# An mLSTM cell followed by a squared-ReLU feed-forward block: loads of later chunks, one chunk's normalisation and the in-place turns of x at other points of the instruction order

## The chip, the core and the metric

The kernel runs on one core of one Trainium2 chip. The metric is the device time of one execution in microseconds (us). A core has five engines that run side by side and meet through semaphores: PE (TensorE, the matmuls; its weight loads are listed as PEld), DVE (VectorE), ACT (ScalarE), POOL (GpSimd) and SP (SyncE, which here issues nearly all DMAs). Each engine works through its own list of instructions in the order in which the kernel's source issues them; an instruction that waits holds up all that stand behind it on the same engine. DMAs issued by SP are carried out by 16 DMA engines.

## The reference

```python
# mLSTM cell: batch 4, 8 heads, 768 steps, head dimension 40
for t in range(S):
    kt, vt, qt = (k[:, :, t], v[:, :, t], q[:, :, t])
    m_new = np.maximum(f_gate[:, :, t] + m, i_gate[:, :, t])
    f_stab = np.exp(f_gate[:, :, t] + m - m_new)
    i_stab = np.exp(i_gate[:, :, t] - m_new)
    m = m_new
    C = f_stab[:, :, None, None] * C + i_stab[:, :, None, None] * np.einsum('bhd,bhe->bhde', vt, kt)
    n = f_stab[:, :, None] * n + i_stab[:, :, None] * kt
    h_tilde = np.einsum('bhde,bhe->bhd', C, qt)
    nq = np.einsum('bhd,bhd->bh', n, qt)[:, :, None]
    denom = np.maximum(np.abs(nq), 1.0)
    o = 1.0 / (1.0 + np.exp(-o_gate[:, :, t]))
    y[:, :, t] = o * h_tilde / denom
# bridge: (4, 8, 768, 40) -> x of 3072 tokens x 320, then the feed-forward block, d_ff = 2048
h = np.maximum(x @ w_in, 0.0)
out = (h * h @ w_out).astype(np.float32)
```

## The kernel before

The 768 steps of each of the 4 batches are cut into 6 chunks of 128 steps, 24 chunks s = 0 to 23 in all. For each chunk the recurrence is worked out in matrix form: scores of k and q, weighted by decays (`W_sb`), times the values, plus the state C carried from chunk to chunk. Its result is normalised and gated into x, 128 tokens by 320. Two chunks make a token group g = s // 2 of 256 tokens, 12 groups in all, which goes through the feed-forward block: `ffn1` (x times w_in, L649 and L660), ReLU on ACT (L675), a square on DVE (L682), and the product with w_out (L743).

No scheduler reorders the work: the source writes out one order by hand, and each engine's list is that order. The first six chunks and the loading of the weights come first. From group g = 1 on, which starts at about 139 us, the order is a list `parts`, walked by n, and **a section of 8 parts belongs to each g** (r = n % 8 is the part in the section, b = 7 + 2 * (n // 8) a chunk number; g = 1 has n = 8 to 15 and b = 9, g = 2 has n = 16 to 23 and b = 11):

- parts 0 and 1: `ffn2_fast` steps 0 and 1 of group g
- parts 2 to 5: the four quarters of `ffn1` for group g + 2, with the scores and the attention of chunks b and b + 1 and b + 2 between them (`tiled`)
- parts 6 and 7: `ffn2_fast` steps 2 and 3 of group g

The sections of g = 10 and 11 have no `ffn1`. Before each part the source issues what stands ahead of it (chiefly work of DVE), and after it what stands behind it.

**`ffn2_fast`** makes the two row blocks y1 and y0 of group g with seven products in place of eight (sums of the squared activations, `sums`, L738, and of w_out, T). A product is 8 matmuls, 16 records in the trace. Products are written into PSUM tiles (`h_ps`), copied by ACT (L763, L768) or added by DVE (L759) into the tiles `y_sb`. There are three buffers of `y_sb`, used in turn: y1 of a group takes one, y0 the next. So y0 of group g + 1 lies in the buffer that y1 of group g had, and its first add (step 0) comes after the landing of y1's store. y1 is stored at the end of step 2 (L779, part 6), y0 at the end of step 3 (L784, part 7). The second product of step 1 overwrites a PSUM tile that the add of y0 in step 0 reads, and the products of steps 1 and 3 write to others that adds read.

**A chunk's way from attention to x** goes by DRAM, since it needs turns across partitions. `attend_turned(s)` leaves the numerators in `tn`; `store_num(s)` (L557) and `load_num(s)` (four DMAs, L562) bring them back in another arrangement. `normalise_turned(s)` (seven DVE instructions, L574 to L583) makes `x_sb`. `store_rows(s)` (L613) writes it to `x_rows` in DRAM, `load_rows(s)` (four DMAs, L618) reads it in blocks of 32 into a half of `xT` of its group, and `turn_squares(s)` (L625, DVE, in place) turns these blocks. `ffn1` of group s // 2 reads this `xT`; its first matmul of the main part is L649.

**Loads.** `load(s)` loads k and v of a chunk (L296, two DMAs), `load_o(s)` its output gate (L324), `load_A(s)` its decays, spread over the partitions (L334, 512 KB), `pair_up` and `load_squares(s)` bring q and k in 32 x 32 blocks (L287; four DMAs, L309). All of these and the stores stand on SP's list, in the order of the source.

In a section, SP's list before the change runs, from part 5 on: x's store of chunk b, the numerators' store and x's four loads of chunk b, the four loads of numerators of chunk b + 1, k and v of chunk b + 5, the gates of chunks b + 5 and b + 6, then y1's store (part 6), the four L309, y0's store (part 7), a load of A, and in the next section x's store and loads of chunk b + 1.

Of the kernel before, what the change touches and what calls it, by code (L numbers as in the profile page):

```python
# [29 lines left out]
def kernel(  # L30
# [536 lines left out]
    def normalise_turned(s):  # L567
        d = st[s]
        N = d["N"].rearrange("p (g e j r) -> p g e j r", g=2, e=2, r=SQ)
        R = D - SQ  # L570
        den = N[:, :, 1, :, R]
        dm = work.tile([P, H], F32, name="dm")
        dm2 = dm[:].rearrange("p (j g) -> p g j", g=2)
        nc.vector.tensor_scalar(dm2, den, scalar1=-1.0, scalar2=1.0, op0=ALU.mult, op1=ALU.max)  # L574
        nc.vector.tensor_tensor(dm2, dm2, den, op=ALU.max)
        nc.vector.reciprocal(dm[:], dm[:])
        x = d["x"] = work.tile([P, 3 * P], F32, name="x_sb")
        x3 = x[:, :DM].rearrange("p (h d) -> p h d", d=D)
        x4, og = x[:, :DM].rearrange("p (j g d) -> p g j d", g=2, d=D), d["og"].rearrange("p (j g) d -> p g j d", g=2)
        nc.vector.tensor_tensor(x4[:, :, :, :SQ], N[:, :, 0], og[:, :, :, :SQ], op=ALU.mult)  # L580
        nc.vector.tensor_tensor(x4[:, :, :, SQ:], N[:, :, 1, :, :R], og[:, :, :, SQ:], op=ALU.mult)
        nc.vector.tensor_tensor(x3, x3, dm[:].unsqueeze(2).to_broadcast([P, H, D]), op=ALU.mult)
        nc.vector.tensor_copy(x[:, DM:], x[:, DM - KR : DM])  # L583
# [27 lines left out]
    def store_rows(s):  # L611
        t = st[s]["xT"] = xT_half(s).rearrange("p c t -> p (c t)")
        nc.sync.dma_start(x_d[s].rearrange("c t d -> t c d"), st[s]["x"][:].rearrange("p (c d) -> p c d", c=3))  # L613

    def load_rows(s):
        t = st[s]["xT"]
        for r in range(P // SQ):
            nc.sync.dma_start(  # L618
                t[r * SQ : (r + 1) * SQ].rearrange("p (b a) -> p b a", a=SQ),
                x_d[s, :, :, r * SQ : (r + 1) * SQ].rearrange("c (n p) a -> p (c n) a", p=SQ),  # L620
            )
# [104 lines left out]
    def sums(g, ps, which=(1, 2, 3, 4)):  # L726

        if "S" not in st:
            st["S"] = [late.tile([P, NPAIR, P], F32, name=f"S{n}", bufs=1) for n in (1, 2, 4)]
        S1, S2, S4 = (t[:, ps] for t in st["S"])  # L730
        g4 = st["g2", g][:].rearrange("p (f two) t -> p f two t", two=2)[:, ps]
        A11, A12, A21, A22 = (g4[:, :, i, n * P : (n + 1) * P] for n in range(2) for i in range(2))
        for n in which:
            to, a, b, op = {
                1: (S1, A21, A22, ALU.add), 2: (S2, S1, A11, ALU.subtract),
                3: (A21, A11, A21, ALU.subtract), 4: (S4, A12, S2, ALU.subtract),
            }[n]
            nc.vector.tensor_tensor(to, a, b, op=op)  # L738
# [48 lines left out]
    def do(f, s):  # L787
        if 0 <= s < NT:
            f(s)

    def score(s):
        scores(s)
        weighted(s)
# [202 lines left out]
    def masked_W(s):  # L996
        weigh(s, masked=True)

    ALL = slice(0, NPAIR)
    for n, (which, g, i) in enumerate(parts):  # L1000
        s, at = 6 + n // 4, n % 4

        r, b = (n % 8, 7 + 2 * (n // 8)) if n >= 8 else (None, None)
        if n == 5:
            brought.close()
            late = ctx.enter_context(tc.tile_pool(name="late", bufs=1, side="right"))
        if n in (0, 4, 8):
            score(s)
            if n == 4:
                square_half()  # L1010
                square_half()
        if n in (2, 5):
            attend_turned(s)
            decays(s + 1)
            mask(s + 1)
            if n > 4:
                turn_kq(s + 1)
            decay_C(s + 1)
            if s > X_SQ:
                turn_squares(s - 1)  # L1020
            attended(s, early=(n == 5))
        if n == 6:
            scale_q(s + 1)
        if 5 <= n < 8:
            sums_of_weights(n - 5)
        if n == 6:
            sums(1, ALL, (1, 2))
        if n == 8:
            load_squares(10)
            load_A(10)  # L1030
            sums_of_weights(3)
            sums(1, ALL, (3,))
        if n == 9:
            score(9)
            attend_turned(8)
            decay_C(9)
            attended(8)
            turn_squares(7)

        if r == 0 and g > 1:  # L1040
            do(turn_squares, b - 2)
            sums(g, ALL, (3,))
        elif r == 4:
            do(scale_q, b + 1)
            do(turn_kq, b + 2)
        elif r == 5:
            do(normalise_turned, b)
            do(store_rows, b)
        elif r == 7 and g < NG - 1:
            sums(g + 1, ALL, (2,))  # L1050
        if g == NG - 2 and which == 2 and i == 3:
            sums(g + 1, ALL, (2,))
        if which == 2 and g == NG - 1 and i == 0:
            sums(g, ALL, (3,))

        if which == 1:
            ffn1_main(g, i)
            if i % 2 == 0:
                st["held"] = st["half"]
            elif r is None:  # L1060
                ffn1_batch(g, i)
                if n != 3:
                    square_half()
                    square_half()
            else:
                x = b + i // 2

                def tiled():
                    do(score, x + 1)
                    do(attend_turned, x)  # L1070

                ffn1_batch(g, i, tiled)
                do(decay_C, x + 1)
        elif g == 0:
            ffn2(g, *divmod(i, 2))
        else:
            ffn2_fast(g, i)

        if n in (2, 6):
            masked_W(s + 1)  # L1080
            if n < 4:
                turn_kq(s + 1)
                scale_q(s + 1)
            normalise_turned(s)
            store_rows(s)
            if n == 2:
                load_squares(s + 2)
            load_rows(s)
            if n == 2:
                load_A(s + 2)  # L1090
        if n == 7:
            for t in range(8, 12):
                sigmoid(t)
            decays(9)
            mask(9)
            turn_kq(9)
        if n == 8:
            masked_W(9)
        elif n == 9:
            load_A(11)  # L1100
            load_o(12)
            load_o(13)
            decays(10)
            mask(10)
        elif n == 10:
            normalise_turned(8)
            store_rows(8)
        if r == 0 and g > 1:
            do(decays, b + 1)
            do(mask, b + 1)  # L1110
            square_half()
            do(normalise_turned, b - 1)
            do(store_rows, b - 1)
        elif r == 1:
            if g > 1:
                do(load_rows, b - 1)
                do(pair_up, b + 2)
            square_half()
            if g < NG:
                sums(g, ALL, (4,))  # L1120
            do(scale_q, b)
            do(turn_kq, b + 1)
        elif r == 2:
            do(masked_W, b + 1)
            do(load_squares, b + 2)
            if n == 10:
                load_rows(8)
        elif r == 3:
            do(decays, b + 2)
            do(mask, b + 2)  # L1130
            attended(b)
            if b % 4 == 3:
                for t in range(b + 1, min(b + 5, NT)):
                    sigmoid(t)
        elif r == 4:
            square_half()
            square_half()
            do(masked_W, b + 2)
            do(load_A, b + 3)
            if b > 9:  # L1140
                do(turn_squares, b - 1)
        elif r == 5:
            do(store_num, b + 1)
            do(load_rows, b)
            do(load_num, b + 1)
            do(load, b + 5)
            for t in range(b + 5, min(b + 7, NT)):
                load_o(t)
        elif r == 6:
            do(load_squares, b + 3)  # L1150
            if n == 14:
                turn_squares(8)
        elif r == 7:
            do(load_A, b + 4)
        if which == 2 and g == NG - 1 and i == 0:
            sums(g, ALL, (4,))
        if n < 5:
            while rounding.done < LAST[n]:
                rounding.step(ahead=rounding.done + 1 < LAST[2])
# [30 lines left out]
```

## Time and profile before

| | us |
|---|---|
| median of 4 runs | 529.32 (528.5 to 534.61) |
| the profiled execution's own time | 528.5 |
| its span, first to last instruction | 526.7 |
| PE busy | 509.9 (97%) |
| PEld busy | 449.0 (85%) |
| DVE busy | 333.3 (63%) |
| ACT busy | 193.4 (37%) |
| POOL busy | 90.1 (17%) |
| DMA packets on SP's queue, share of 16 engines' span | 60.4% |
| granted clock of TensorE, mean | 0.993 |

The profile is of one execution. Its times are counted from the span's start. A row of the waits reads: who waited, for whom, us in total, times, longest. A row of the timeline reads: start, length, engine, line, operation, what is written and read, and in brackets how long the engine sat idle before and what ended that. Rows of SP are the issues of DMAs; a DMA lands some us after its issue. A row of the stretches reads: from and to, length, busy time of each engine with the number of instructions, the granted share of TensorE's clock, and the DMA engines' share and rate.

### The profile page before, as it was taken

Reading aid. Unit: us, or ns where it says so; the run is one execution under the profiler, and the core shown is the slowest. Engines: PE = TensorE matmul, PEld = TensorE weight load, DVE = VectorE, ACT = ScalarE, POOL = GpSimd, SP = SyncE. Lnnn points to the kernel's source line nnn. Section 1 sums busy time; section 2 is a strip of 40 time slices with the busy share of each in tenths; the row PEclk is TensorE's granted clock in tenths of the full one; section 3 lists DMA queues with packets and bytes.
Section 4 is the critical chain, followed back from the end, with each engine's and each line's share of the span. In section 5 each row is a group of like instructions: output and inputs, shape, how many; then the busy total and the mean of one; then the engine's idle time right before and its main releaser. Section 6 shows DMA issues by size and latency. Waiting matters only on the chain.

```text
span 526.7 us, 10339 instructions
## 1 busy us (share of the span) xinstructions
PE 509.9 (97%) x3933; PEld 449.0 (85%) x3933; DVE 333.3 (63%) x638; ACT 193.4 (37%) x460; POOL 90.1 (17%) x110
## 2 busy tenths in 40 slices
PE   9998999989999979999999999989999999999997
PEld 5876788877888878998898888988898898998997
DVE  8579988679866644754855845745865864431451
ACT  3786587362644123532334422333522301102000
POOL 3346553232321100010210211000210100000000
PEclk9999999999999979999999999999999999999999
DMA  9999698877679584785684774775664221200000
GB/s 196 227 201 210 149 201 200 191 175 149 149 152 180 138 167 78 167 143 112 168 147 101 172 135 110 178 137 118 148 153 75 72 79 36 64 12 1 26 26 26
DMA packets 239394, 68.06 MB, mean 129 GB/s; under 512 B 185744, under 2 KB 233872, under 8 KB 239344
## 3 DMA queue, kind: packets, MB, share of 16 engines
q1 hardware_dynamic: 239248, 67.20, 60.4%
q8 instruction: 31, 0.51, 0.4%
q10 hardware_dynamic: 96, 0.20, 0.1%
q14 instruction: 19, 0.16, 0.1%
HBM read 55.08 MB, written 17.86 MB: 138 GB/s over the span
## 4 chain that ended last, share of the span: by engine, by line
PE 64%; DMA 12%; SPq 11%; DVE 6%; ACT 3%; issue 3%; POOL 1%; DVEq 0%; POOLq 0%; ACTq 0%
PE h_ps L649 22%; PE h_ps L743 19%; PE h_ps L660 6%; DMA x_rows<-x_sb 4%; PE h_ps L689 3%; PE tp L424 3%; DMA out_dram<-y_sb 3%; SPq L562 3%; SPq L618 2%; SPq L324 2%; SPq L309 2%; PE numT L534 2%; DMA num_rows<-tn 1%; PE idle L802 1%; ACT W_sb L383 1%
## 5 line engine op out<-in xcount | busy, mean ns | idle before, releaser
L649 PE MATMUL h_ps<-xT,w_in 128*128 128x256 f32 x768 | 173.1, 383 | 1.8 <-POOL w_in L215 0.9
L649 PEld LDWEIGHTS h_ps<-xT,w_in 128*128 128x128 f32 x768 | 144.5, 191 | 23.5 <-issue 1.4
L675 ACT ACTIVATE r_sb<-h_ps 128x512 f32<-128x512 f32 x96 | 49.8, 599 | 112.0 <-PE h_ps L660 58.1
L743 PE MATMUL h_ps<-w_out,g 128*128 128x160 f32 x528 | 79.1, 306 | 6.3 <-DVE y_sb L759 6.2
L743 PEld LDWEIGHTS h_ps<-w_out,g 128*128 128x128 f32 x528 | 75.0, 194 | 7.8 <-DVE y_sb L759 7.5
L682 DVE TENSOR_TENSOR g<-r_sb 128x512 f32<-128x512 f32 x96 | 66.4, 741 | 10.0 <-ACT r_sb L675 10.0
L383 ACT ACTIVATE W_sb<-A_bc,b_T 128x128 f32<-128x128 f32 x176 | 53.8, 388 | 24.6 <-POOL A_bc L359 24.4
L437 DVE TENSOR_TENSOR P_sb<-tp,W_sb 128x512 f32<-128x512 f32 x46 | 29.7, 685 | 51.2 <-PE numT L534 33.5
L743 PE MATMUL h_ps<-T,S 128*128 128x160 f32 x352 | 52.3, 302 | 0.0
L743 PEld LDWEIGHTS h_ps<-T,S 128*128 128x128 f32 x352 | 48.8, 190 | 1.6 <-issue 0.9
L660 PE MATMUL h_ps<-xT,w_in 64*128 64x256 f32 x384 | 49.0, 391 | 0.0
L660 PEld LDWEIGHTS h_ps<-xT,w_in 64*128 64x128 f32 x384 | 34.8, 186 | 12.1 <-issue 9.1
L759 DVE TENSOR_TENSOR y_sb<-y_sb,h_ps 128x160 f32<-128x160 f32 x44 | 14.1, 320 | 44.4 <-PE h_ps L743 44.4
L763 ACT COPY y_sb<-h_ps 128x160 f32<-128x160 f32 x11 | 3.2, 293 | 99.5 <-PE h_ps L743 99.5
L359 POOL TENSOR_SCALAR_AFFINE_SELECT A_bc<-A_bc 128x1024 f32<-128x1024 f32 x22 | 27.2, 1236 | 73.5 <-ACT kq L369 64.3
L396 POOL TENSOR_TENSOR vw<-va,W_sb 128x328 f32<-128x328 f32 x20 | 17.4, 870 | 76.2 <-ACT W_sb L383 62.4
L490 POOL TENSOR_TENSOR Cd<-C,kq 128x164 f32<-128x164 f32 x15 | 6.9, 463 | 120.0 <-DVE C L551 105.7
L759 DVE TENSOR_TENSOR y_sb<-h_ps,y_sb 128x160 f32<-128x160 f32 x11 | 3.6, 324 | 37.1 <-DMA out_dram<-y_sb 23.8
L424 PEld LDWEIGHTS tp<-kqT 40*128 40x128 f32 x384 | 24.8, 188 | 2.4 <-issue 1.1
L743 PE MATMUL h_ps<-w_out,S 128*128 128x160 f32 x176 | 25.8, 300 | 0.8 <-DVE y_sb L759 0.8
L424 PE MATMUL tp<-kqT 40*128 40x128 f32 x384 | 26.1, 275 | 0.0
L743 PE MATMUL h_ps<-T,g 128*128 128x160 f32 x176 | 25.7, 299 | 0.0
(119 smaller groups left out, 609.7 us busy)
## 6 DMA issues: line engine op xcount, KB each, us to landing
A_bc<-a_rows SPq DMA_DIRECT2D x23, 512.0 KB, 4.9
raw<-in_moe_w_out_dram SPq DMA_DIRECT2D x16, 320.0 KB, 3.8
num_rows<-tn SPq DMA_DIRECT2D x18, 256.0 KB, 2.4
kq<-num_rows SPq DMA_DIRECT2D x72, 64.0 KB, 2.1
kqT<-kq_rows SPq DMA_DIRECT2D x34, 128.0 KB, 3.1
raw<-in_moe_w_in_dram SPq DMA_DIRECT2D x8, 512.0 KB, 5.2
kq<-in_k_dram SPq DMA_DIRECT2D x24, 160.0 KB, 3.9
va<-in_v_dram SPq DMA_DIRECT2D x24, 160.0 KB, 4.6
```

The source lines that it names most:

```text
L359: nc.gpsimd.affine_select(A[:], A[:], compare_op=ALU.is_ge, fill=-1e30, base=0, pattern=[[0, H], [1, P]], channel_multiplier=-1,)
L383: nc.scalar.activation(d["W"][:, i * n + h, :], A[i][:, h, :], AF.Exp, bias=b_T[:, b, c, i * n + h : i * n + h + 1],)
L396: nc.gpsimd.tensor_tensor(d["vw"][:], d["va"][:], d["W"][:, :, P - 1 : P].to_broadcast([P, H, D1]), op=ALU.mult,)
L424: nc.tensor.matmul(sc[i][:, j, :], lhsT=d["kT"][rows, j, :], rhs=d["qT"][rows, j, :], start=True, stop=True,)
L437: nc.vector.tensor_tensor(t, d["sc"][i], d["W"][:, heads, :], op=ALU.mult)
L562: nc.sync.dma_start(N[m * SQ : (m + 1) * SQ].rearrange("p (e c) -> p e c", c=P), n_d[s, :, m * P : (m + 1) * P].rearrange("(e p) c -> p e ...
L649: nc.tensor.matmul(hs[i][:, n, :], lhsT=w_in[:, a, fb * P : (fb + 1) * P], rhs=xT[:, :, a, :], start=(n == 0 and a == 0), stop=False,)
L660: nc.tensor.matmul(hs[i][:, n, :], lhsT=w_in2[rows, 2 * pp + n, :], rhs=xT[rows, :, 2, :], start=False, stop=(n == 1),)
L675: nc.scalar.activation(rs[-1][:], h[:], AF.Relu)
L682: nc.vector.tensor_tensor(g4[:, :, i, :], r[:], r[:], op=ALU.mult)
L743: nc.tensor.matmul(to, lhsT=lhsT[:, p], rhs=rhs[:, p, :], start=(start and p == 0), stop=(p == NPAIR - 1), skip_group_check=True,)
L759: add = lambda to, a, b: nc.vector.tensor_tensor(to, a, b, op=ALU.add)
```

## The change

Three things change places in the written order; no instruction is added or taken away.

- `load(b + 5)` and the two `load_o` go from the end of part 5 to the end of part 6, and so behind y1's store (L779) on SP's list. This is in effect in sections that still have chunks to load, g = 1 to 5.
- For chunk 9 alone, `normalise_turned` and `store_rows` go from ahead of part 5 in section g = 1 (n = 13) to behind part 6 (n = 14), and its `load_rows` from behind part 5 to behind part 7 (n = 15).
- `turn_squares(b - 2)` goes from ahead of part 0 to ahead of part 1 of a section, and the sum (3) stays ahead of part 0. On DVE's list the turn now stands behind the add of y0, two squares and the normalisation of chunk b - 1. `turn_squares(8)` stays in part 6 and stands behind chunk 9's normalisation there.

```diff
@@ ahead of a part
         if r == 0 and g > 1:
+            sums(g, ALL, (3,))
+        elif r == 1 and g > 1:
             do(turn_squares, b - 2)
-            sums(g, ALL, (3,))
         elif r == 4:
             do(scale_q, b + 1)
             do(turn_kq, b + 2)
-        elif r == 5:
+        elif r == 5 and b > 9:
             do(normalise_turned, b)
             do(store_rows, b)
@@ behind a part
         elif r == 5:
             do(store_num, b + 1)
-            do(load_rows, b)
+            if b > 9:
+                do(load_rows, b)
             do(load_num, b + 1)
+        elif r == 6:
+            if n == 14:
+                normalise_turned(9)
+                store_rows(9)
             do(load, b + 5)
             for t in range(b + 5, min(b + 7, NT)):
                 load_o(t)
-        elif r == 6:
             do(load_squares, b + 3)
             if n == 14:
                 turn_squares(8)
         elif r == 7:
             do(load_A, b + 4)
+            if n == 15:
+                load_rows(9)
```

SP's list in the changed kernel, from y1's store of section g = 1 to x's loads of chunk 9: L779, L613 (x of chunk 9), two L296, two L324, four L309, L784, L334, four L618 (x of chunk 9); then L613 and four L618 of chunk 10.

## The prediction

> **What bounds the kernel now.** I read the page's busy shares, then the waits of TensorE alone, then the busy time of each engine in chosen stretches, then the SP queue and the chain of waits where TensorE stands still.
>
> ```profile
> PE 509.9 (97%) x3933; PEld 449.0 (85%) x3933; DVE 333.3 (63%) x638; ACT 193.4 (37%) x460; POOL 90.1 (17%) x110
> ```
> ```profile
> PE h_ps L743 <- DVE y_sb L759: 7.0, 5, 3.2
> ```
> ```profile
> DVE y_sb L759 <- DMA out_dram<-y_sb: 23.8, 5, 5.4
> ```
>
> TensorE is busy for 97% of the span: time can only come from its gaps or from clock lost behind them. From 130 us on it waits for one thing alone, 5 times, 7.0 us: the adds of y (L759), which wait for the landing of an earlier store of y (23.8 us in 5 waits). A section's y0 takes the buffer that the section before stored as y1, through L779. The stretches below are part 1 of sections g = 2 to 7 (32 matmul records), then the halves behind the longest gap; the columns are the length, busy time by engine, the granted clock, DMA share and GB/s.
>
> ```profile
> 186.83:196.83 10.00, 6.76 (x35) 6.52 (x34) 3.74 (x11) 2.63 (x9) 0.91 (x1) 0.75 0.91 166
> 231.35:236.19 4.84, 4.62 (x34) 4.38 (x33) 2.55 (x9) 2.44 (x9) 0.70 (x1) 1.00 1.01 163
> 270.76:275.46 4.70, 4.62 (x35) 4.38 (x33) 2.56 (x9) 2.30 (x8) 0.65 (x1) 1.00 0.85 142
> 310.03:315.70 5.67, 4.61 (x34) 4.37 (x33) 2.55 (x9) 2.64 (x9) 0.00 (x0) 1.00 1.03 166
> 349.37:355.67 6.30, 4.61 (x34) 4.37 (x33) 2.55 (x9) 2.65 (x9) 0.69 (x1) 1.00 0.94 163
> 390.25:394.59 4.34, 4.34 (x34) 4.34 (x33) 3.10 (x10) 1.95 (x7) 0.64 (x1) 1.00 0.50 151
> ...
> 192.40:196.83 4.43, 4.43 (x17) 4.43 (x18) 3.14 (x9) 2.23 (x8) 0.91 (x1) 0.50 0.85 165
> 196.83:204.69 7.86, 7.86 (x34) 6.48 (x33) 4.42 (x6) 0.00 (x0) 0.00 (x0) 0.89 0.47 110
> ```
>
> Undisturbed, part 1 takes 4.34 us (g = 7, whose predecessor has no k, v or gates to load). In g = 2 it takes 10.00: 3.24 us of gap, then half clock. The clock is 0.50 for 4.43 us and 0.89 over the next 7.86, which is 1.73 us more at half: 6.16 us at half speed, 3.08 us lost, for a gap of 3.24. The gap of 1.69 us in g = 6 cost no clock. Why the store lands late is seen in SP's queue at the end of section g = 1:
>
> ```profile
> 183.61 1.84 SPq L562 DMA_DIRECT2D kq<-num_rows  x4
> 185.54 0.39 SPq L296 DMA_DIRECT2D kq<-in_k_dram  x1
> 186.04 0.53 SPq L296 DMA_DIRECT2D va<-in_v_dram  x1
> 186.62 2.43 SPq L324 DMA_DIRECT2D og<-in_o_gate_dram  x2
> 189.15 0.86 SPq L779 DMA_DIRECT2D out_dram<-y_sb  x1
> 190.06 2.90 SPq L309 DMA_DIRECT2D kqT<-kq_rows  x4
> 193.06 0.51 SPq L784 DMA_DIRECT2D out_dram<-y_sb  x1
> 193.67 0.38 SPq L334 DMA_DIRECT2D A_bc<-a_rows  x1
> 195.70 0.37 SPq L613 DMA_DIRECT2D x_rows<-x_sb  x1
> ```
>
> The add that L779 needs is done by 181.7, yet the store is issued at 189.15 and lands 2.75 us later by the chain, behind the loads of k, v and gates.
>
> **Loads behind the store (sections g = 1 to 5).** Nothing is added: L779 passes two L296 and two L324, 3.6 us of issue (185.54 to 189.15). The store lands about 3 us sooner, and the longest gap in g = 3 to 6 is 1.69. The four excesses over 4.34 go: 0.50 + 0.36 + 1.33 + 1.96 = 4.15 us gained. The loads come 0.4 to 0.9 us later; the values are first multiplied more than a section of 39 us on, so this costs nothing, and even without that cover less than 1 us a section. Bounds are 3.6 and 4.15: in g = 5 the store could be issued at 346.1, where k's load was, and even with the longest landing of the view, 4.5 us, it is there at 350.6, ahead of 351.7, where TensorE came to stand; I allow 0.1 us of waiting left in each of five.
>
> **Tenth chunk (s = 9), on VectorE.** Its seven instructions (L574 to L583, 175.44 to 177.25, 1.8 us) leave the place where they waited 3.81 us for their load, ahead of chunk 11's weighting. The store of the numerators (L557) needs only the weighting and the turn behind these, and goes from 179.28 to about 176.9. The add of part 6 no longer holds TensorE for 0.83 us: the product of 177.04 to 180.20 takes 3.16 us against 2.18 elsewhere, 0.98 gained. In the new place, 1.8 us behind part 6's last add, turn and S2 (0.5 + 1.2) end at about 183.3, and the product that reads S2 starts at 183.5: covered by 0.2 us; if not, some tenths.
>
> So TensorE reaches the first matmul of ffn1 in section g = 2 at 196.83 - 5.66 (10.00 less 4.34) - 0.98 = 190.2. It reads xT of chunks 8 and 9.
>
> **Tenth chunk, on the SP queue.** One store of x (L613) and four loads (L618, 1.86 us) move; the queues of POOL and ACT issue nothing here. Before, the loads are issued at 181.65 and chunk 9's turn ends at 185.95. Now L613 stands behind L779, and the four L618 behind L613, k, v, two gates, four L309, L784 and A's load. I walk the queue. L557 at 176.9 follows A_bc (issued 176.27) through the DMA engines, landing about 181.4, since A_bc landed at 181.1 with more beside it; four L562 end at 183.3; L779 is issued at 183.3 and lands before 186, y0's add needing it at 185.9 and TensorE at 187.9. From the end of L562 to A's load the queue took 193.67 - 185.45 = 8.2 us; with L613's 0.4 this is 191.9. The four L618 are issued from 192.4 to 194.3. They can't land before A: a median of 4.9 us from issue (section 6 of the page), 196.8; chunk 10's x store, issued at 195.70 behind an A of 193.67, released its loads at 199.10, 0.5 us after that A's 4.9. Their 196 KB add about 1 us at the 166 GB/s of that stretch: 197.8. Turn and two handovers, 0.7: 198.5.
>
> [...]
>
> So TensorE stands from 190.2 to 198.5, 8.3 us, a longer gap than the one removed; VectorE's turn waits with part 1's add, two squares, S4, the scaling of q and a turn behind it, some 4.8 us of work that scores at 209 need: covered. The price of clock: nothing (as behind 1.69 us) to 3.1 us (as behind 3.24 us); nearest is the second, so 3.1. The 32 matmuls, 7.00 us elsewhere, end at 198.5 + 7.0 + 3.1 = 208.6 instead of 204.69: 3.9 us lost, all earlier gains in this section counted.
>
> [...]
>
> Bounds: if the DMA engines hold up no issue (both gates at 0.6, as at 160.93, 1.2 us less; four L309 at 0.45, 1.1 less) and x lands 1.8 us after its last issue (xT's least), the turn ends at 194.0; with 4.2 (xT's longest) and a queue 1 us later, at 200.5. With 0 to 3.1 of clock the local change runs from 3.7 us won to 5.9 lost.
>
> **An x turn a part later (g = 2 to 9).** The 0.57 us of L625 move behind y0's add, two squares and a normalisation. Section g = 7 shows what there is between them and TensorE's need:
>
> ```profile
> 390.50 0.33 DVE L759 TENSOR_TENSOR y_sb<-h_ps,y_sb 128x160 f32<-128x160 f32 x1 [2.49 <-PE h_ps L743]
> 390.74 1.29 DVE L682 TENSOR_TENSOR g<-r_sb 128x512 f32<-128x512 f32 x2
> 393.55 0.20 DVE L583 COPY x_sb<-x_sb 128x64 f32<-128x64 f32 x1
> ...
> 394.59 0.59 PE L649 MATMUL h_ps<-xT,w_in 128*128 128x256 f32 x2
> ```
>
> The turn would run from 393.7 to 394.3, 0.3 us ahead of L649: nothing lost, 0 to 0.3 in each of six sections as bounds (1.8).
>
> **Sum.** The profiled execution took 528.5 us: a span of 526.7 and 1.8 around it. 528.5 - 4.15 + 3.9 = 528.3. The median of the four runs shown is 529.32, 0.8 above this execution, so no change that a run could tell; a measurement here tells about 1% (5.3 us).
>
> **Rivals.** (a) Chunk 9 is no obstacle: xT is turned by 190.2. Then 6.64, the 0.86 us of clock in L649 and 4.15 are won: 516.9. Against it: eleven DMAs stand between L779 and the first L618. (b) The queue runs freely, turn at 194.0: a gap of 3.8 us, matmuls done at 204.1 with 3.1 of clock, 0.6 won there: 523.8; without the loss of clock 520.7. For it: the store of numerators is out of the tangle; against it: a DMA share of 0.91 in that stretch. (c) Slower: the turns hold TensorE in each section. A normalisation in part 0 that waits for its numerators passes each us over 0.3 on to L649. VectorE has waited 5 times, 12.0 us, for such loads; five waits of 2.4 us, less 0.3 each, cost 10.5: 538.8. It decides from a wait of 0.3 us on. Against it: all five waits stood at other parts, none in part 0.
>
> **How the numbers follow.** Forecast 0.70, (a) 0.05, (b) 0.13, (c) 0.12. The forecast's own range is 524.5 to 531.5 (both ends of xT and of clock, not all at once). The range, 523.5 to 532.0, takes in (b) with its clock and leaves out (a), (c) at its full price and (b) without, about 0.2. Faster by over 1% means under 524.0: (a) and most of (b), 0.15. Slower by over 1%, over 534.6: 0.11, most of (c). Within: 0.74.
>
> **What would show it.** Right: part 1 at 4.34 us in g = 3 to 6; L779 at about 183; the first L649 of g = 2 waits some 8 us for L625, which waits for xT, and the clock halves again there. Wrong: no wait of PE for xT (a, b), or gaps ahead of L649 in later sections (c), or y's adds that still wait for out_dram.

## The result, and the profile after

| | before | after |
|---|---|---|
| median us (runs) | 530.82 (64) | 532.81 (43) |
| lowest to highest | 524.22 to 535.72 | 529.70 to 537.09 |
| ratio, 95% interval | | 1.0059 (1.0044 to 1.0074) |

The ratio leaves out as slow the runs more than 1.5% above their kernel's fastest, 19 of before's 64 and none of after's; over all runs the medians lie 2.0 us apart, 0.4%. So the change made the kernel slower by 0.4 to 0.6%, 2.0 to 3.1 us, where the prediction's sum had 0.2 gained. The profiled execution of after took 534.48 us, its span 532.7. First the busy shares of its page:

```profile
PE 513.7 (96%) x3933; PEld 450.5 (85%) x3933; DVE 332.8 (62%) x638; ACT 194.4 (36%) x460; POOL 91.8 (17%) x110
```

The waits of TensorE from 130 us on (who waited, for whom, us in total, times, longest):

```profile
PE h_ps L649 <- DVE xT L625: 10.6, 2, 9.8
PE h_ps L743 <- DVE y_sb L759: 0.5, 2, 0.3
```

The wait for y's adds has all but gone, from 7.0 us to 0.5; among VectorE's waits the adds wait for a store of y twice, 7.1 us in all, where it was 5 times, 23.8. In its place stands one wait of 9.8 us for the turned x, and a small one. The stretches of after: part 1 of g = 2, 3 and 6, and the first 32 matmuls of `ffn1` in g = 2 (length, busy time by engine, granted clock, DMA share, GB/s):

```profile
188.74:203.59 14.85, 4.78 (x34) 4.29 (x32) 4.15 (x12) 2.64 (x9) 0.78 (x1) 0.81 0.85 159
239.65:243.99 4.34, 4.34 (x34) 4.34 (x33) 3.65 (x11) 1.94 (x7) 0.69 (x1) 1.00 1.16 144
...
356.18:361.54 5.36, 4.51 (x35) 4.27 (x33) 3.65 (x12) 2.74 (x9) 0.69 (x1) 1.00 1.04 185
203.59:212.97 9.38, 9.38 (x32) 7.64 (x32) 4.25 (x6) 0.00 (x0) 0.00 (x0) 0.75 0.54 89
```

Part 1 takes the undisturbed 4.34 us in g = 3 (4.35 in g = 4 and 5), but 14.85 in g = 2, and 5.36 in g = 6. SP's list shows where the 9.8 us come from (start, length, line, what is written and read):

```profile
185.80 1.74 SPq L562 DMA_DIRECT2D kq<-num_rows  x4
187.64 0.38 SPq L779 DMA_DIRECT2D out_dram<-y_sb  x1
188.12 1.63 SPq L613 DMA_DIRECT2D x_rows<-x_sb  x1
...
192.68 3.51 SPq L309 DMA_DIRECT2D kqT<-kq_rows  x4
...
197.98 2.21 SPq L618 DMA_DIRECT2D xT<-x_rows  x4
```

x of chunk 9 is stored at 188.12, and its loads are issued only at 197.98, behind ten other DMAs. The last of these, A's load, is issued at 197.55 and lands at 201.87; the four loads of x land from 202.24 to 202.88. So x landed behind A, as the prediction's walk had it: in the profiles of before and after each of SP's 471 DMAs lands behind the one issued before it (neighbours on the list report through different ones of eight semaphores, so the order can be read). VectorE's turn and TensorE's list show the rest (idle time before, and what ended it, in brackets):

```profile
202.96 0.58 DVE L625 STREAM_TRANSPOSE xT<-xT 128x384 f32<-128x384 f32 x1 [8.30 <-DMA xT<-x_rows]
```
```profile
203.59 9.45 PE L649 MATMUL h_ps<-xT,w_in 128*128 128x256 f32 x32 [9.77 <-DVE xT L625]
```

Where the 6.0 us between the two spans went, counted from the first product of a section's part 1 to the next one's:

| us | before | after | difference | predicted |
|---|---|---|---|---|
| start to part 1 of g = 1 (same instructions in the same order) | 146.6 | 149.4 | +2.8 | 0 |
| g = 1 and 2 (chunk 9, first longer gap) | 84.76 | 90.25 | +5.5 | +3.9 |
| g = 3 to 6 | 158.90 | 156.57 | -2.3 | -4.15 |
| from part 1 of g = 7 to the end of the products | 133.3 | 133.3 | 0 | 0 |

The first row is not the change's. Without it the two executions differ by 3.2 us, the 0.6% of the ratio; a second profile of each (e9, e10) gives 376.8 and 380.1 us for that stretch, against 377.0 and 380.2. Before's stretch isn't that short in every execution: e7, which has the order of before from part 1 of g = 1 on, took 383.8 us for it, on a chip where the median of before is 534.34, with 12.1 us of waits for y.

### The profile page after: what moved, and what is told of

Read it like the earlier page. It is cut to its first block, busy times and chain, and to the rows that moved or that the text cites. A ratio compares the mean times of both kernels' runs of the same rounds, so it can differ in the third digit from the quotient of the medians.

```text
span 532.7 us, 10333 instructions
## 1 busy us (share of the span) xinstructions
PE 513.7 (96%) x3933; PEld 450.5 (85%) x3933; DVE 332.8 (62%) x638; ACT 194.4 (36%) x460; POOL 91.8 (17%) x110
## 5 line engine op out<-in xcount | busy, mean ns | idle before, releaser
L649 PE MATMUL h_ps<-xT,w_in 128*128 128x256 f32 x768 | 177.6, 390 | 12.5 <-DVE xT L625 10.6
L649 PEld LDWEIGHTS h_ps<-xT,w_in 128*128 128x128 f32 x768 | 147.3, 195 | 36.0 <-DVE xT L625 11.4
L743 PE MATMUL h_ps<-w_out,g 128*128 128x160 f32 x528 | 75.8, 300 | 0.3 <-DVE y_sb L759 0.3
L743 PEld LDWEIGHTS h_ps<-w_out,g 128*128 128x128 f32 x528 | 72.9, 190 | 0.8 <-DVE y_sb L759 0.6
L743 PE MATMUL h_ps<-T,S 128*128 128x160 f32 x352 | 52.3, 302 | 0.0
L743 PEld LDWEIGHTS h_ps<-T,S 128*128 128x128 f32 x352 | 48.7, 190 | 1.6 <-issue 0.9
L359 POOL TENSOR_SCALAR_AFFINE_SELECT A_bc<-A_bc 128x1024 f32<-128x1024 f32 x22 | 28.6, 1301 | 81.2 <-ACT kq L369 76.7
L316 DVE STREAM_TRANSPOSE kqT<-kqT 128x1024 f32<-128x1024 f32 x17 | 21.0, 1237 | 10.6 <-DMA kqT<-kq_rows 10.5
L424 PEld LDWEIGHTS tp<-kqT 40*128 40x128 f32 x384 | 24.8, 188 | 2.6 <-issue 1.4
L424 PE MATMUL tp<-kqT 40*128 40x128 f32 x384 | 26.3, 276 | 0.0
L369 ACT ACTIVATE kq<-A_bc 64x512 f32<-64x512 f32 x30 | 18.8, 628 | 20.4 <-DMA A_bc<-a_rows 18.6
L743 PE MATMUL h_ps<-w_out,S 128*128 128x160 f32 x176 | 25.8, 300 | 0.2 <-DVE y_sb L759 0.2
```

The lines of the kernel that those rows point to most:

```text
L316: nc.vector.transpose(t, t)
L359: nc.gpsimd.affine_select(A[:], A[:], compare_op=ALU.is_ge, fill=-1e30, base=0, pattern=[[0, H], [1, P]], channel_multiplier=-1,)
L369: nc.scalar.activation(e[rows], st[s]["A"][0][rows, PR * i : PR * (i + 1), :], AF.Exp)
L424: nc.tensor.matmul(sc[i][:, j, :], lhsT=d["kT"][rows, j, :], rhs=d["qT"][rows, j, :], start=True, stop=True,)
L649: nc.tensor.matmul(hs[i][:, n, :], lhsT=w_in[:, a, fb * P : (fb + 1) * P], rhs=xT[:, :, a, :], start=(n == 0 and a == 0), stop=False,)
L743: nc.tensor.matmul(to, lhsT=lhsT[:, p], rhs=rhs[:, p, :], start=(start and p == 0), stop=(p == NPAIR - 1), skip_group_check=True,)
```

## The experiments

Three parts can be made apart: L (the loads behind the store), C (chunk 9's normalisation and its x's DMAs) and T (the turn a part later). The theory "Queue" is the prediction's: L wins, C loses by its place on SP's list, T is free. Its rivals are in the expectations.

**e1_loads_late: before with L alone.**

```diff
             do(load_num, b + 1)
+        elif r == 6:
             do(load, b + 5)
             for t in range(b + 5, min(b + 7, NT)):
                 load_o(t)
-        elif r == 6:
             do(load_squares, b + 3)
```

> Only the loads of k, v and gates go behind y1's store; chunk 9 and the turns stay as before. Three theories of why the change cost 3 us where the sum said none. Queue: chunk 9's x loads, behind eleven DMAs on SP's list, cost some 12 us (9.8 of waiting, 2.3 of clock) and the rest of the change wins. VectorE: the turns a part later hold TensorE. DMA: loads pushed later collide with what follows and slow it. Queue and VectorE expect here that the gaps ahead of part 1's second half go (5.7 us and 0.9 of clock in section g = 2, 2 to 4 in g = 3 to 6): 7 to 11 us under the kernel before, ratio 0.980 to 0.987. DMA expects under 3 us won, ratio above 0.994.

Measured: 524.23 us, ratio 0.9897 (0.9859 to 0.9935). The waits of TensorE in e1:

```profile
PE h_ps L743 <- DVE y_sb L759: 2.3, 5, 1.0
```

The longest wait is 1.0 us, no stretch of half clock stands in the sections (the 6.83 us near 50 us alone make the mean clock 0.993), and g = 2 takes 38.26 us instead of 44.53. L is a gain of 1.0%: 6.2 us between the medians on that chip, where Queue expected 7 to 11 and the theory "DMA" under 3. It doesn't clear all five gaps: 2.3 us are left. The loads do push back what stands behind them: VectorE waits 22.6 us in eight places for the blocks of q and k (L316), where it was 3.4 in two. What that costs TensorE isn't shown.

**e2_turn_late: before with T alone.**

```diff
         if r == 0 and g > 1:
-            do(turn_squares, b - 2)
             sums(g, ALL, (3,))
+        elif r == 1 and g > 1:
+            do(turn_squares, b - 2)
```

> Only the turns of x go a part later; loads and chunk 9 stay as before. Queue: within 1 us of the kernel before, ratio 0.998 to 1.002, since in the profile before the turn would end 0.3 us ahead of the matmul that needs it; but where the add of y0 is late by a late store, the turn behind it is late as well, so up to 3 us more, some tenths in each of g = 3 to 6. VectorE: 3 us or more slower, ratio 1.006 or above, with TensorE waiting ahead of L649 in most sections.

Measured: 536.59 us, ratio 1.0116 (1.0084 to 1.0148). "T is free" fell. The waits of TensorE in e2:

```profile
PE h_ps L743 <- DVE y_sb L759: 6.8, 4, 3.3
PE h_ps L649 <- DVE xT L625: 5.5, 6, 1.4
```

The second row is new; the first stays as before. In section g = 6 of e2:

```profile
360.53 0.33 DVE L759 TENSOR_TENSOR y_sb<-h_ps,y_sb 128x160 f32<-128x160 f32 x1 [5.94 <-DMA out_dram<-y_sb]
...
364.12 0.56 DVE L625 STREAM_TRANSPOSE xT<-xT 128x384 f32<-128x384 f32 x1
364.74 2.00 PE L649 MATMUL h_ps<-xT,w_in 128*128 128x256 f32 x8 [1.39 <-DVE xT L625]
```

y0's add is late by the store of y and lets TensorE go on at 360.91. From then on VectorE needs 3.6 us to the turn (two squares, seven instructions of the normalisation), and the turn 0.56 more: 4.2 us with the handover from add to L649's start. TensorE's products need less, 2.44 us. So the late store is paid twice, once ahead of L743 and once, by 1.4 us, ahead of L649. The numerators were in time; it is not they that make the turn late.

**e12_turn_ahead_of_normalisation: before with the turn behind the add and the squares, but ahead of the normalisation.**

```diff
         if r == 0 and g > 1:
-            do(turn_squares, b - 2)
             sums(g, ALL, (3,))
...
             square_half()
+            do(turn_squares, b - 2)
             do(normalise_turned, b - 1)
```

> The kernel before, with only the turn of x moved, as in the second experiment, but not as far: behind y0's add and two squares and ahead of the normalisation of chunk b - 1 (seven instructions, 1.8 us). The second experiment was 1.2% slower with six waits for L625 of up to 1.4 us. If the normalisation in front of the turn is the cause (where y0's add is late by a late store, TensorE needs xT 2.2 us behind it, and the squares, normalisation and turn take 3.6), the waits go, ratio 0.998 to 1.003. If a turn behind y0's add is late anyway, or the earlier place of the sum is the cause, it stays at 1.008 or above.

Measured: 531.99 us, ratio 1.0001 (0.9968 to 1.0035). From 130 us on TensorE has one row of waits:

```profile
PE h_ps L743 <- DVE y_sb L759: 10.0, 6, 3.8
```

The adds hold TensorE even longer than in e2 (10.0 us against 6.8), and yet L649 doesn't wait for L625. Behind the late add the turn held TensorE by up to 1.4 us with the normalisation (1.8 us) between them (e2), and nowhere without it (e12). That settles e2's 1.2%.

**e3_loads_and_turn: L and T, chunk 9 as before.** The edits of e1 and e2 together.

> Loads behind the store and turns a part later; chunk 9 stays as before. This is the change without its move of chunk 9. Queue: the wait of 9.8 us for xT in section g = 2 is gone, ratio 0.980 to 0.990, within 1.5 us of the run with the loads alone. VectorE: 3 us or more slower than the loads alone. DMA: about the kernel before, ratio above 0.994.

Measured: 524.57 us, ratio 0.9890 (0.9856 to 0.9923), level with e1. With the stores early T costs nothing that these runs can tell, against the theory "VectorE", though its profile has waits for the turn that e1 lacks:

```profile
PE h_ps L649 <- DVE xT L625: 2.1, 3, 1.4
PE h_ps L743 <- DVE y_sb L759: 2.1, 3, 1.2
```

So the whole change without C is 1.1% faster than before, and C takes it to 0.4 to 0.6% slower: some 8 to 9 us. (In the two profiles it is 8.6 us, 371.6 against 380.2 from part 1 of g = 1 to the end of the products.)

**e4_chunk9_and_turn: C and T, the loads as before.** After, with `load` and `load_o` put back to the end of part 5.

```diff
             do(load_num, b + 1)
+            do(load, b + 5)
+            for t in range(b + 5, min(b + 7, NT)):
+                load_o(t)
...
-            do(load, b + 5)
-            for t in range(b + 5, min(b + 7, NT)):
-                load_o(t)
             do(load_squares, b + 3)
```

> Chunk 9's moves and the turns a part later; the loads stay ahead of y1's store as before. Queue: TensorE stands for xT of chunk 9 as long as in the changed kernel (8 to 10 us, then half clock) and nothing is won in g = 3 to 6, so 4 to 8 us slower than before, ratio 1.008 to 1.016, 2 to 4 us slower than the changed kernel. DMA: the loads are in their old place, so no slower than before, ratio 0.997 to 1.003.

Measured: 540.87 us, ratio 1.0191 (1.0155 to 1.0227), more than Queue's 1.016. The waits of TensorE in e4:

```profile
PE h_ps L649 <- DVE xT L625: 9.4, 5, 4.4
PE h_ps L743 <- DVE y_sb L759: 7.0, 4, 3.8
```

On top of T alone, C costs only 1.0191 / 1.0116 = 1.007, not 1.015 to 1.017. Its wait for xT in g = 2 is 4.4 us where after's is 9.8: TensorE comes to ffn1 late there, held by y's store, and the two waits overlap. The parts don't add: L is worth 1.0% alone and 1.3 to 1.5% ahead of C and T (after's 1.0059, or 1.0037 by the medians, over 1.0191), and what L clears in g = 2 is what uncovers C.

**e5_x_loads_early: after with x's four loads of chunk 9 directly behind x's store.**

```diff
                 store_rows(9)
+                load_rows(9)
             do(load, b + 5)
...
-            if n == 15:
-                load_rows(9)
```

> The changed kernel, with the four loads of chunk 9's x issued directly behind its store, ahead of k, v, gates, the four block loads, y0's store and A's load. Queue: SP now waits some 3 us for x's store to land, then x is in xT about 6 us sooner than in the changed kernel; the wait ahead of L649 in section g = 2 falls from 9.8 to 2 to 4 us with at most one window of half clock: 8 to 10 us under the changed kernel, ratio to the kernel before 0.987 to 0.993. If the wait is not the place on the queue but the way of chunk 9 as such (late normalisation, store, turn), the wait stays at 8 us or more and the ratio at 1.003 or above. SP's own wait of 3 us could make later loads late: then up to 2 us are given back.

Measured: 532.19 us, 534.34 for before on that chip, ratio 0.9967 (0.9942 to 0.9992): better than after, less than expected. (The expectations' window of half clock is 3.41 us, half of the stretch of 6.83 in before.) SP's list in e5:

```profile
186.04 0.38 SPq L613 DMA_DIRECT2D x_rows<-x_sb  x1
190.04 1.85 SPq L618 DMA_DIRECT2D xT<-x_rows  x4
```

L618 reads what L613 writes, so SP itself waits for the store to land: 3.6 us in which nothing behind them is issued. The wait for xT in g = 2 fell to 2.3 us, but k, v, gates and squares went out later, and TensorE now waits 5.1 us in four places for turns, this one among them, and 2.4 us ahead of L424.

**e11_x_loads_behind_gates: the same loads behind the gates' loads, ahead of the four L309.**

```diff
                 load_o(t)
+            if n == 14:
+                load_rows(9)
             do(load_squares, b + 3)
...
-            if n == 15:
-                load_rows(9)
```

> The changed kernel, with chunk 9's four x loads behind the gates and ahead of the four block loads, y0's store and A's load: six DMAs fewer in front of them, and SP should not have to wait, since in the changed kernel x's store lands at 191.5 and the gates are issued until 192.6. Queue: x lands near 196.5 in place of 202.9, the wait ahead of L649 falls from 9.8 to 3 to 4 us with at most 6.83 us of half clock: 5 to 8 us under the changed kernel, ratio to the kernel before 0.991 to 0.997. If the six DMAs are not what it waits for, the ratio stays above 1.002.

**e10_changed_again: after itself, on the same chip.**

> The changed kernel, unchanged, on the same chip as the two beside it, so that they can be compared. Ratio to the kernel before 1.004 to 1.008; a wait of 8 to 11 us ahead of L649 in section g = 2 and two or three windows of half clock behind it.

Measured: e11 527.56 us, ratio 0.9923 (0.9891 to 0.9955); e10 531.85 us, ratio 1.0043 (1.0011 to 1.0075), where the median of before on that chip is 530.64. The two differ by where four loads stand among ten. The wait of TensorE for the turn, first in e10, then in e11, and SP's list in e11:

```profile
PE h_ps L649 <- DVE xT L625: 10.7, 3, 9.4
```
```profile
PE h_ps L649 <- DVE xT L625: 5.6, 2, 4.2
```

```profile
186.63 0.38 SPq L613 DMA_DIRECT2D x_rows<-x_sb  x1
...
190.06 2.63 SPq L618 DMA_DIRECT2D xT<-x_rows  x4
192.74 2.69 SPq L309 DMA_DIRECT2D kqT<-kq_rows  x4
```

SP doesn't wait here: the loads of k, v and gates fill the time that x's store needs to land. L618 is issued 3.4 us behind L613 instead of 9.9 (after), the wait for xT falls from 9.4 us (e10) to 4.2, and 4.3 us come back between the two medians, 0.8%. The order of the list fits that: in after the loads of x stand behind A on it and land behind it, from 202.24 on against 201.87, while in e11 they are issued at 190.06, ahead of A at 196.14.

**e6_gap_filled: after with 42 matmuls on zeros ahead of `ffn1` in g = 2,** so that TensorE is busy while xT is on its way.

```diff
+        if n == 18:
+            idle(42)
         if which == 1:
```

> The changed kernel with 42 small matmuls on zeros (0.22 us each at full clock, 9 us) ahead of the first matmul of ffn1 in section g = 2, in the gap in which TensorE stands for xT. They do no work. If the half clock behind the gap costs 2.3 us, as the profile of the changed kernel says (4.66 us at half behind the gap), the first 32 matmuls take 7.0 to 7.4 instead of 9.38 us and the run is 1.5 to 2.5 us under the changed kernel, ratio to the kernel before 1.000 to 1.004. If the clock costs nothing that isn't hidden, it stays at 1.006; if the small matmuls end later than xT is there, it is slower than the changed kernel.

Measured: 533.78 us, ratio 0.9978 (0.9953 to 1.0003) on the chip of e5. TensorE in e6:

```profile
193.56 9.14 PE L802 MATMUL idle<-zeros 128*128 128x512 bf16 x41
204.18 7.17 PE L649 MATMUL h_ps<-xT,w_in 128*128 128x256 f32 x32 [1.47 <-DVE xT L625]
```

The 32 matmuls of L649 end 7.1 us after their start, not 9.38, and 7.11 us is what 32 of them take at full clock (at 248.0 in before): the price of the clock behind the gap is 2.3 us. The ratio is a little better than expected; after was not run beside it, so how much of the 0.8% against after's 1.0059 is the chip's stays open. A gain of the whole kernel isn't shown: from part 1 of g = 1 to the end of the products e6 takes 380.3 us, after 380.2.

**e7, e8, e9: where the prediction's base came from.** Of 14 profiles taken in all, part 1 of g = 1 starts anywhere from 146.3 to 149.7 us. Near 50 us after, e1 to e4 and e9 show 6.83 us at half clock, which the profile of before used by the prediction lacks. e7 is before, e8 is e1, each with a few matmuls on zeros ahead of the gaps there; e9 is before once more.

```diff
             else:
+                if u == 2:
+                    idle(6)
                 turn_rows(s - 1)
```

> The kernel before, with 6 small matmuls on zeros ahead of the third turn of x in the first part, where TensorE stands 1.5 us and 0.9 us within 5 us. In the five profiles of other kernels taken so far this pair of gaps was followed by 6.83 us at half clock near 50 us; in the profile of the kernel before it was not, and that execution was 2.3 us under its median. If that is why, the median goes down by 2 to 3.4 us, ratio 0.9935 to 0.996, and no half clock stands near 50 us. If the spread of the runs has another cause, the ratio is 0.999 to 1.002.

> The loads of k, v and gates behind y1's store alone, as in the first experiment, with the 6 small matmuls of the kernel beside it. If both effects stand for themselves, the first experiment's 0.990 less 0.004 to 0.006: ratio 0.983 to 0.987. If the half clock near 50 us has no price, 0.990.

> The kernel before, unchanged, for another profiled execution. The prediction's sum was made against an execution of 528.5 us whose clock was at half only behind the gap of section g = 2 (mean 0.993); most executions of it have a mean clock of 0.984 to 0.990. If that is what made the base low, this profile shows 6.83 us or more at half clock in the first part too, near 50 us, and a span of 528 to 533. If it shows none there and yet a longer span, the base differs by something else, such as longer gaps at the stores of y.

Measured: e7 534.71 us, ratio 1.0016 (0.9983 to 1.005): no gain. TensorE's wait of 1.5 us ahead of L633, the first of the two gaps, is not among its waits, and part 1 of g = 1 started at 148.6, no earlier. That the half clock there makes the base late is thereby not shown. e8 528.13 us, ratio 0.9879 (0.9840 to 0.9918): not to be told from e1. e9, one execution: 529.64 us, part 1 of g = 1 at 147.9, half clock at 49.0 for 6.83 us, TensorE's waits for y 8.0 us in five. What sets the start of g = 1 in an execution stays open.

## Why the prediction was right or wrong

**What failed, in short.** The median of after, 532.81, lies 4.5 us above the forecast of 528.3. The base makes 2.3 of them, and by the medians the change 2.2 (+2.0 against -0.2). In the two profiles the change cost 3.2 us where 0.25 were to be won, and two terms make nearly all of the difference: in g = 3 to 6 2.3 us were won instead of 4.15, and in g = 1 and 2 5.5 were lost instead of 3.9, since the walk of the queue was too short. Inside the first lies the one step that was wrong in kind: the turn of x, put at nothing, holds TensorE for 0.85 us in g = 6.

**The base: wrong, by 2.3 us.** The sum started from one execution's 528.5 us. The median of 64 runs is 530.82. The text set 528.5 beside a median of four runs and let the difference of 0.8 be. The range ended at 532.0, 0.8 us short. Part of the spread is the chip's: the medians of before in the three sets of experiments were 530.4, 534.3 and 530.6.

**Loads behind the store: right in mechanism, size halved in g = 3 to 6.** Part 1 takes 4.34 or 4.35 us in g = 3, 4 and 5 as said. But the sections won 0.49, 0.35, 0.65 and 0.84 us, where 0.50, 0.36, 1.33 and 1.96 were written. In g = 5 0.68 is missing: 0.15 stands in a gap, the rest is spread over products elsewhere in the section, so the gap's removal was partly given back there. In g = 6 1.12 is missing, and the trace names it:

```profile
357.75 0.33 DVE L759 TENSOR_TENSOR y_sb<-h_ps,y_sb 128x160 f32<-128x160 f32 x1 [4.19 <-DMA out_dram<-y_sb]
...
361.54 0.48 PE L649 MATMUL h_ps<-xT,w_in 128*128 128x256 f32 x1 [0.85 <-DVE xT L625]
```

The store of y is issued at 355.69 there, behind four loads of numerators (L562) whose issue took 2.97 us against 1.74 in g = 1, and lands at 357.6. The add is late, and with it the turn. The prediction allowed 0.1 us a section for a store that is still late, and none for what stands behind the add.

**x turn a part later: the step wrong in kind.** "Nothing lost, 0 to 0.3 in each" was read from g = 7, a section in which the add waits for no store. There the margin is 0.3 us. In g = 2 to 6 of before the add does wait for a store (23.8 us in five waits, as the prediction itself shows), and where it is late all that stands behind it on VectorE's list is late, L625 now among it. e2 puts the price at 1.2% where stores are late, e3 at nothing that its median tells where L has moved them, and after pays 0.85 us in g = 6, where a store is still late. Rival (c) had the place right (turns that hold TensorE by more than 0.3 us) and the trigger wrong: it had the numerators' loads in mind, and it is the store of y.

**Tenth chunk on SP's queue: right in mechanism.** The first L649 of g = 2 waits for L625, which waits for xT, behind the eleven DMAs, and the clock halves again. The times read side by side:

| | predicted | after | 
|---|---|---|
| L779 issued | 183.3 | 187.64 |
| x's loads issued | 192.4 to 194.3 | 197.98 to 200.2 |
| TensorE at ffn1 | 190.2 | 193.83 |
| wait for xT | 8.3 | 9.77 |
| clock lost behind it | 3.1 | 2.4 |

About 3 us of each time is the later start (162.91 against 165.91 at the same matmul of g = 1). L779 was 1.3 us later than that since A's load and the numerators' store went out later than walked; the rest of the queue then took 10.3 us from L779 to L618 against 9.1 predicted. TensorE came 0.6 later than that as well. From that matmul to the end of the 32 of L649 before took 41.78 us and after 47.07: +5.3, where +3.9 was predicted. The 1.4 us between them are 1.5 of longer wait and 0.6 of later arrival, less 0.7 of clock: the term mis-sized is the walk of the queue. Counted from the later start, the turn ended at 200.5, the late bound that the prediction named (its own terms, 194.3 + 1 + 4.2 + 0.7, make 200.2). The 0.98 us that part 6 should win came: 1.09 from that matmul to part 1.

**The clock: between the two.** In after TensorE runs at half speed from 198.0 to 208.25, 10.24 us, of which 4.66 lie behind the gap: 2.4 us lost, by e6 2.3. The prediction took the second of its two values, nothing (as behind 1.69 us) and 3.1 (as behind 3.24 us); in before 6.16 us at half speed fell on matmuls, here 4.66, and the other 5.6 us lay in the gap.

**Rivals (a) and (b)**, xT in time or the queue free, did not happen. With six fewer DMAs ahead (e11) TensorE still waited 4.2 us for xT.

**The versions beside it.** e1, e3 and e8 (ratios 0.9897, 0.9890, 0.9879) are faster than both kernels and not to be told apart. The loads behind the store are what is worth keeping; chunk 9's part is what made the change lose.

## What to carry to other kernels

In the traces of before and after all 471 DMAs of SP's list landed in the order of their issue: a load that is moved back is priced by all that it now stands behind (9.77 us of waiting behind ten DMAs in after), and where it reads what a store wrote, independent loads between the two fill the wait (e11, where SP issues on without a gap) while none between them makes the queue itself wait (e5, 3.6 us). A margin is read in the section where what comes before is late (0.85 us of waiting in g = 6 of after), not in the quiet one (0.3 us to spare in g = 7 of before); instructions that stand behind a late event in an engine's list hand its lateness on, so what is needed first goes first behind it (ratio 1.0001 in e12 against 1.0116 in e2). A base for a forecast at the level of 1% is a median of many executions, on the chip on which the change will be measured.

## What the runs showed of the hardware

Half clock came in stretches of 3.41 us (e9), 6.83 (before, after, e9) and 10.24 (after), one, two and three times the same length, the last stretch (2.5 us in before, 2.2 in after), cut by the end of the kernel, aside. The stretch does not follow from the gap's length: 6.83 us at the 3.24 of before, 3.41 at 3.4 at the same place in e9, 10.24 around the 9.77 of after.

The same gaps came with it and without. Near 50 us two gaps follow each other: 1.50 and 0.88 us in before, without half clock; 1.51 and 0.85 in after, with 6.83 us of it from 51.2 on; 1.5 and 0.2 in e9, with 6.83 from 49.0 on. The stretch behind them in the prediction's profile of before, and then in e9 (granted clock after the five busy times):

```profile
52.00:56.00 4.00, 4.00 (x28) 3.14 (x26) 3.93 (x7) 1.70 (x6) 2.70 (x2) 1.00 0.31 87
```
```profile
52.00:56.00 4.00, 4.00 (x11) 3.17 (x10) 3.96 (x6) 1.52 (x6) 3.06 (x2) 0.52 0.35 96
```

28 matmul records at full clock in the first, 11 at 0.52 in the second, for the same instructions in the same order. A forecast from one profile takes one side of that.

The same issue on SP takes different times, for a reason that the runs don't show: the two gates' loads took 1.59 us in after, 2.65 in e1 and 2.43 in before, x's store 1.63 us in after and 0.38 in e11.
